# Turning K and Q in place to free 2 KB for half a streamed weight unit

One change to a tuned kernel: a memory-augmented recurrent attention whose weights do not all fit on the core.

## Chip, cores, metric

One core of a Trainium2 chip. The metric is device time in microseconds (us) of the whole kernel; lower is better. Engines are TensorE (PE; its weight loads PEld), VectorE (DVE), ScalarE (ACT), GpSimd (POOL), SyncE (SP) and 16 DMA engines. A verdict of faster or slower needs 2%.

## The reference

```python
def _A_ref(x, mem0, Wq, Wk, Wv, Wo, seg_len):       # S = 2048, Dm = 1024, H = 32, Dh = 128, M = 8, seg = 32
    mem = mem0
    for s in range(n_seg):                          # 64 segments, one after the other
        h = concatenate([mem, x[segment s]])        # 8 + 32 rows
        q, k, v = h @ Wq, h @ Wk, h @ Wv            # each Dm x (H Dh)
        p = softmax(where(mask, q k^T * scale, -1e9))
        o = (p v) @ Wo
        mem = o[:M]                                 # the next segment starts from this
        outs.append(o[M:])
# _B_ref: gelu(x @ w1 + b1) @ w2 + b2;  result: x + A(layernorm(x)) + B(layernorm(x))
```

Segments depend on each other through `mem`, and each needs all four matrices of 8 MB.

## The kernel before

The weights are 64 units of 512 KB: K, Q and V in halves of 8 units (K0, Q0, K1, Q1, V0, V1), then O with 16 units of two heads each. SBUF holds 46 of them all the time. Of the other 18, one waits in PSUM and 17 are read again from HBM in every segment, through six buffers:

```python
def start_stream():
    ...
        t = slab(STREAM_PLACES[started % STREAM_BUFS])             # one of six 4 KB-per-partition buffers
        if streams[started] == IN_PSUM and "kept" in nxt:
            ...                                                    # the unit kept in PSUM, copied by VectorE
        else:
            nc.sync.dma_start(out=t[:, :], in_=copies[streams[started]])
        stream_tiles.append(t); started += 1
def unit_done(unit):
    if IS_STREAMED[unit]:
        start_stream()                                             # a used unit's buffer takes the next transfer
        ...
```

A segment's own 32 rows are 8 memory rows and 24 rows x; the last 8 rows of four segments ("left-over rows", hL) are projected together, once per four segments, K in segments with s mod 4 = 0, Q in 1 (unit half 0) and 2 (half 1), V in 3, O in 1. I call these the first, second, third and fourth **kind** of segment. K and Q leave PSUM through one shared home, `nat_home`, and are turned from there by VectorE:

```python
def rows_out(ps, out, cp): cp(out=out, in_=ps.rearrange("p (h e) -> p h e", e=32)); let_go(ps)
def turn(out):             nc.vector.transpose(out=out, in_=nat_home)
def turn_k():              st["kT"] = sp.tile([P, 16, 32], BF16, name="kT", tag="a"); turn(st["kT"][:, :, :])
def turn_kL(ps, u):        rows_out(ps, nat_home, nc.vector.tensor_copy); kL[u] = ...; turn(kL[u][:, :, :])
def turn_q(ps):            rows_out(ps, nat_home, nc.scalar.copy); turn(q_home[:, :, NL:40])
...
psK1, psK1L = half_pass("K", 1, left_k, {})
rows_out(psK1, nat_home, nc.scalar.copy)
at = {0: [lambda: scores(0), turn_k], 6: [lambda: sums(0)]}        # after unit 0 / unit 6 of the Q1 pass
if left_k:
    at[1] = [lambda: turn_kL(psK1L, 1)]
psQ1, psQ1L = half_pass("Q", 1, left_q[1], at)
turn_q(psQ1)
```

`scores(u)` makes the products of Q and K on TensorE, the exponential `pr` on ScalarE (L745) and the mask on VectorE (L750); `sums(u)` divides by the row sums (TensorE first, L758). L628 are the products of K, Q and V, L808 those of O, L250 the cast that ends the memory's path to the next segment.

The softmax here doesn't subtract the row's maximum and nothing guards it: scores larger than these inputs give would overflow.

## Time and profile before

Runs of this kernel vary by over 1%: over four calls its single runs lie between 1996 and 2025 us, all of the same state, with medians of 2014.0, 2011.5, 2011.8 and 2011.5. A difference between two kernels of under 5 us needs the many rounds that the experiments have.

| what | before |
|---|---|
| time, median | 2014.7 us |
| TensorE busy | 1779 us, 88% |
| DMA, 600 to 1900 us | share 1.00, 383 GB/s |

In the lists of waits a row reads: engine and line, what ended the wait, total us, times, longest. In the stretches a row reads: from:to, length, then busy us and instruction count of each engine, the granted clock, DMA share, GB/s. The prediction shows the lines, and splits the 158 us for which TensorE is idle.

### The profile page before, as it was taken

To read this page: it belongs to the slowest core of one execution; us is meant where nothing else is said; L and a number is where in the kernel's file an instruction comes from. 1 tells how busy PE (TensorE), PEld (TensorE's weight loads), DVE (VectorE), ACT (ScalarE), POOL (GpSimd) and SP (SyncE) were. 2 spreads that over 40 slices of the span, in tenths; PEclk is the share of its full clock that TensorE was granted. 3 is DMA by queue.
4 is the path that set the end of the run, shared out by engine and by line. 5 is a ranking of instruction groups with operands and counts; after the bars stand their busy time and mean duration, and the time that the engine had idled before them with its cause. 6 is when DMAs were issued, how large, how long until landed. Compare 5 with 4: busy or idle time off the path is not lost.

```text
span 2011.7 us, 77091 instructions
## 1 busy us (share of the span) xinstructions
PE 1779.0 (88%) x34291; PEld 978.6 (49%) x34291; DVE 862.9 (43%) x2232; ACT 590.2 (29%) x1349; POOL 280.1 (14%) x544
## 2 busy tenths in 40 slices
PE   6999999988688988898889888888888989888887
PEld 3444444444344455545555545555545445554443
DVE  6656566333243444343434434334434343434332
ACT  4343434212222222222222222222222322222222
POOL 0000000002331111111111111111111111111111
PEclk9999999999999999999999999999999999999999
DMA  9821212779899999999999999999999999999998
GB/s 329 262 53 44 55 41 55 285 286 399 329 364 380 390 385 374 380 383 379 389 383 384 389 364 384 392 369 385 373 380 376 391 364 390 390 401 389 388 381 308
DMA packets 227402, 661.13 MB, mean 329 GB/s; under 512 B 48107, under 2 KB 63387, under 8 KB 227068
## 3 DMA queue, kind: packets, MB, share of 16 engines
q1 hardware_dynamic: 207324, 636.04, 83.5%
q0 software_dynamic: 16512, 17.92, 2.7%
q8 instruction: 268, 4.39, 0.9%
q10 hardware_dynamic: 3232, 2.25, 0.3%
q14 instruction: 66, 0.54, 0.1%
HBM read 641.85 MB, written 31.52 MB: 335 GB/s over the span
## 4 chain that ended last, share of the span: by engine, by line
PE 58%; DMA 29%; issue 5%; DVE 4%; ACT 2%; POOL 1%; SPq 0%; DVEq 0%; ACTq 0%; POOLq 0%
PE acc L628 26%; DMA u<-Wc_O 13%; PE ps L430 10%; PE acc L808 8%; PE ps L478 7%; DMA u<-Wc_V 6%; DMA res<-hr_d 3%; DMA u<-Wc_Q 2%; PE ps L511 2%; DMA outL_d<-res 2%; PE mixed L783 1%; ACT d_oL L671 1%; DVE b_oL L684 1%; DVE d_oL L671 1%; PE acc L783 1%
## 5 line engine op out<-in xcount | busy, mean ns | idle before, releaser
L628 PE MATMUL acc<-u,hr 128*32 128x512 bf16 x11520 | 792.7, 382 | 47.2 <-DMA u<-Wc_V 15.0
L628 PEld LDWEIGHTS <-hr 128*32 128x32 bf16 x12288 | 356.4, 97 | 311.1 <-issue 71.0
L671 ACT CAST d_oL<-acc 128x512 bf16<-128x512 f32 x256 | 150.3, 587 | 443.0 <-PE acc L628 354.1
L628 PE MATMUL acc<-u,hrL 128*32 128x512 bf16 x2880 | 259.6, 389 | 8.0 <-issue 8.0
L430 PE MATMUL ps<-u 128*128 128x512 bf16 x896 | 195.7, 381 | 2.6 <-ACT u L327 2.6
L808 PEld LDWEIGHTS <-b_oL 128*32 128x32 bf16 (+1 forms) x3552 | 117.0, 104 | 109.7 <-issue 76.4
L808 PE MATMUL acc<-u,d_oL 128*32 128x256 bf16 (+1 forms) x2220 | 134.2, 294 | 34.4 <-DMA u<-Wc_O 20.9
L684 DVE STREAM_TRANSPOSE kT<-d_oL 128x512 bf16<-128x512 bf16 x128 | 90.6, 708 | 160.4 <-ACT d_oL L671 157.1
L808 PE MATMUL acc<-W_O,b_oL 128*32 128x256 bf16 (+1 forms) x2220 | 135.8, 307 | 22.5 <-issue 22.5
L478 PE MATMUL ps<-u 128*128 128x512 bf16 x672 | 147.0, 379 | 0.0
L808 PEld LDWEIGHTS <-d_oL 128*32 128x32 bf16 (+1 forms) x3552 | 102.8, 98 | 86.6 <-issue 63.1
L430 PEld LDWEIGHTS <-u 128*128 128x128 bf16 x896 | 88.0, 98 | 109.0 <-issue 4.8
L808 PE MATMUL acc<-u,b_oL 128*32 128x256 bf16 (+1 forms) x1332 | 96.9, 311 | 34.7 <-DMA u<-Wc_O 28.9
L684 DVE STREAM_TRANSPOSE b_oL<-d_oL 128x512 bf16<-128x512 bf16 x128 | 91.1, 712 | 73.3 <-ACT d_oL L671 70.8
L628 PEld LDWEIGHTS <-hrL 128*32 128x32 bf16 x3072 | 89.5, 98 | 63.2 <-issue 25.0
L213 DVE COPY u<-kept 128x1024 bf16<-128x1024 bf16 x126 | 81.2, 686 | 73.5 <-PE acc L808 54.8
L796 DVE CAST b_oL<-acc 128x160 bf16<-128x160 f32 x128 | 41.6, 325 | 163.6 <-PE acc L789 163.6
L478 PEld LDWEIGHTS <-u 128*128 128x128 bf16 x672 | 65.3, 98 | 77.4 <-DVE g_u L446 0.4
L223 POOL DMA_DIRECT2D hr<-hr_d x63 | 34.6, 549 | 489.5 <-PE acc L628 405.3
L948 POOL DMA_DIRECT2D out_dram<-res x124 | 63.5, 517 | 260.3 <-DVE res L910 259.0
L438 ACT ACTIVATE g_xb<-ps,b1col 128x512 bf16<-128x512 f32 x112 | 76.9, 687 | 60.6 <-PE ps L430 59.5
L893 ACT CAST d_oL<-acc 128x256 bf16<-128x256 f32 x63 | 23.5, 372 | 235.2 <-PE acc L808 207.7
(130 smaller groups left out, 2148.9 us busy)
## 6 DMA issues: line engine op xcount, KB each, us to landing
u<-Wc_O SPq DMA_DIRECT2D x384, 512.0 KB
u<-Wc_K SPq DMA_DIRECT2D x256, 512.0 KB
u<-Wc_V SPq DMA_DIRECT2D x256, 512.0 KB
u<-Wc_Q SPq DMA_DIRECT2D x193, 512.0 KB
u<-in_B_w_dram SPq DMA_DIRECT2D x16, 448.0 KB
u<-in_B_w_dram SPq DMA_DIRECT2D x14, 512.0 KB
u<-in_A_Wq_dram SPq DMA_DIRECT2D x12, 512.0 KB
u<-in_A_Wv_dram SPq DMA_DIRECT2D x12, 512.0 KB
```

The costliest lines, as they stand in the source:

```text
L213: nc.vector.tensor_copy(out=t[:, 1024 * b:1024 * b + 1024], in_=nxt["kept"][:, b, :])
L430: nc.tensor.matmul(ps[:, :].rearrange("p (s t) -> p s t", t=SEG), lhsT=w1_sb[fb // 14 * 8 + kt][:, (fb % 14) * P:(fb % 14 + 1) * P], rhs=x ...
L438: nc.scalar.activation(out=xb[:, :], in_=ps[:, :], func=ACT.Identity, bias=b1col[:, fb:fb + 1], scale=1.0)
L478: nc.tensor.matmul(ps[:, :], lhsT=gts[fc // 4][:, fc % 4, t * P:(t + 1) * P], rhs=w2_sb[fc // 2][:, fc % 2, cs], start=(fc == 0), stop=(fc ...
L511: nc.tensor.matmul(pss[2 * t + nb][:, :], lhsT=gts[fc // 4][:, fc % 4, t * P:(t + 1) * P], rhs=w2_sb[fc // 2][:, fc % 2, nb * 512:nb * 512 ...
L628: nc.tensor.matmul(o, lhsT=lhs[:, i, :], rhs=m, start=(i == seq[0]), stop=(i == seq[-1]), tile_position=(0, 32 * j),)
L671: cp(out=out, in_=ps.rearrange("p (h e) -> p h e", e=32))
L684: nc.vector.transpose(out=out, in_=nat_home)
L783: nc.tensor.matmul(oV[b][:, c, :], lhsT=V[q, c * P:(c + 1) * P], rhs=prA[q, c, :], start=(c == 0), stop=False, skip_group_check=True, tile ...
L796: cp(out=outs[u][:, hs, NL * slot:NL * slot + 40], in_=oV[b])
L808: nc.tensor.matmul(acc[r:r + n // 8, 0:n], lhsT=lhs[:, 4 * (i % 4) + 2 * u + k, :], rhs=t[:, 1024 * k + n * jq:1024 * k + n * jq + n], sta ...
L948: nc.gpsimd.dma_start(out=out_flat[rows, 256 * j:256 * j + 256], in_=res[32 * j:32 * j + NX, :])
```

## The change

Its intent: free 2 KB per partition and keep there one of the two heads of one streamed O unit, so that 256 KB less are read per segment. K and Q are copied straight to where they will lie and turned there; V's home and the residual's buffer go, and the residual is loaded into the buffers of the softmax's weights (`pr`, `pr_last`) once these are used up.

```diff
-SCRATCH = 576
-SMALL = 3520
+SCRATCH = 512
+SMALL = 3584
+HALF = [unit for unit in ORDER[48:] if IS_STREAMED[unit]][0]
...
-    qL = nc.alloc_sbuf_tensor_at("qL", [P, 2, 16, SEG], BF16, offset=SCRATCH)
-    v_home = nc.alloc_sbuf_tensor_at("v_home", [P, 512], BF16, offset=SCRATCH + 2048)
-    pr_last = nc.alloc_sbuf_tensor_at("pr_last", [P, 224], BF16, offset=SCRATCH + 3072)
+    half_home = nc.alloc_sbuf_tensor_at("half_home", [P, DM], BF16, offset=SCRATCH)
+    pr_last = nc.alloc_sbuf_tensor_at("pr_last", [P, 256], BF16, offset=SCRATCH + 2048)
+    qL_last = nc.alloc_sbuf_tensor_at("qL_last", [P, 16, SEG], BF16, offset=SCRATCH + 2560)
...
-                nc.sync.dma_start(out=t[:, :], in_=copies[streams[started]])
+                c0 = 1024 if streams[started] == HALF else 0
+                nc.sync.dma_start(out=t[:, c0:2048], in_=copies[streams[started]])
...
-            def turn(out):
-                nc.vector.transpose(out=out, in_=nat_home)
+            def turn(ps, home, cp):
+                rows_out(ps, home, cp)
+                nc.vector.transpose(out=home, in_=home)
...
-            rows_out(psK1, nat_home, nc.scalar.copy)
+            turn_k(psK1, 1)
...
-            at = {0: [lambda: scores(0), turn_k], 6: [lambda: sums(0)]}
             if left_k:
-                at[1] = [lambda: turn_kL(psK1L, 1)]
+                turn_kL(psK1L, 1)
+            at = {0: [lambda: scores(0)], 6: [lambda: sums(0)]}
...
-                st["res"] = sp.tile([P, 256], BF16, name="res", tag=tag)       # own buffer in three kinds of four
+                st["res"] = sp.tile([P, 256], BF16, name="res", tag="e")       # the buffer of pr, always
...
+                if n == 7 and left_o:
+                    st["resL"] = pr_last
+                    nc.gpsimd.dma_start(out=st["resL"][:, :], in_=hrL_d[og, :, 256:512])
```

(Cut: the identity and masks move to other buffers; `q_left` now comes before `turn_q`.)

More of the change, by code (lines that the diff above doesn't have):

```diff
@@ L141, in slab @@
         return slabs.tile([P, 2048], BF16, name="u", tag=place)
-    ident = consts.tile([P, P], BF16, name="ident")
-    make_identity(nc, ident[:])
+    qL = [consts.tile([P, 16, SEG], BF16, name="qL"), qL_last]
+    ident = pr_last[:, 0:P]
+    make_identity(nc, ident)
+    ident_mem = consts.tile([P, 4, NL], BF16, name="ident_mem")
+    nc.vector.tensor_copy(out=ident_mem[:, :, :], in_=ident.rearrange("p (j t) -> p j t", j=4)[:, :, NX:SEG])
     bd = consts.tile([P, P], BF16, name="bd")
@@ L150 @@
         nc.vector.memset(bd[q, q], 1.0)
-    mask = qL.rearrange("p u h t -> p (u h t)")[:, 0:NX + GRP * 16]
+    mask = qL_last.rearrange("p h t -> p (h t)")[:, 0:NX + GRP * 16]
     mask_order = mask[:, 0:NX]
@@ L184 @@
     copies = {
-        unit: dram.tile([P, 2048], BF16, name="Wc_" + "_".join(map(str, unit)))[:, :]
+        unit: dram.tile([P, 1024 if unit == HALF else 2048], BF16, name="Wc_" + "_".join(map(str, unit)))[:, :]
         for unit in ORDER if IS_STREAMED[unit]
@@ L190, in fetch @@
         w, i, u = unit
-        if w == "O":
+        if unit == HALF:
+            h = 4 * i + 2 * u
+            nc.sync.dma_start(out=half_home[:, :], in_=Wo_v[:, h, :])
+            nc.sync.dma_start(out=t, in_=Wo_v[:, h + 1, :])
+        elif w == "O":
             h = 4 * i + 2 * u
@@ L237, with put_mem @@
     nat_home, q_home = outs[0][:, :, 32:64], outs[1][:, :, 24:64]
-    def put_mem(o_sb, hT, ps, nb=4, m0=0):
+    def put_mem(o_sb, hT, ps, nb=4):
         nc_ = KT // nb
-        rows = ident[:, :].rearrange("p (j t) -> p j t", j=nb)[:, :, m0 + NX:m0 + SEG]
+        rows = ident_mem[:, :, :] if nb == 4 else ident_mem[:, 1::2, :]
         psM = ps[:, 0:8 * KT].rearrange("p (c j t) -> p c j t", c=nc_, j=nb)
@@ L323, in turn_x @@
             for kt in range(KT):
-                nc.tensor.transpose(pT[:, kt, :], xn[:, kt * P:(kt + 1) * P], ident[:, :])
+                nc.tensor.transpose(pT[:, kt, :], xn[:, kt * P:(kt + 1) * P], ident)
             for half in range(2):
@@ L505 @@
                     nc.tensor.matmul(
-                        pss[n][:, :], lhsT=ident[:, :], rhs=xtoks[4 * tg + n // 2][:, cs], start=False, stop=False
+                        pss[n][:, :], lhsT=ident, rhs=xtoks[4 * tg + n // 2][:, cs], start=False, stop=False
                     )
@@ L565, in keep_unit @@
                 for k in range(4):
-                    nc.tensor.transpose(tr[:, k, :], t[:, 512 * n + P * k:512 * n + P * (k + 1)], ident[:, :])
-                turned = v_home.rearrange("p (k t) -> p k t", k=4)
+                    nc.tensor.transpose(tr[:, k, :], t[:, 512 * n + P * k:512 * n + P * (k + 1)], ident)
+                turned = late.tile([P, 512], BF16, name="VL0").rearrange("p (k t) -> p k t", k=4)
                 nc.vector.tensor_copy(out=turned, in_=tr)
@@ L570, in keep_unit @@
                     c0 = 512 * (n % 2) + P * k
-                    nc.tensor.transpose(kept[:, n // 2, c0:c0 + P], turned[:, k, :], ident[:, :])
+                    nc.tensor.transpose(kept[:, n // 2, c0:c0 + P], turned[:, k, :], ident)
             nxt["kept"] = kept
@@ L680, in left_values, with turn_k @@
                 VL[u] = values_out(ps, late.tile([P, 512], BF16, name=f"VL{u}"), nc.vector.tensor_copy)
-            def turn(out):
-                nc.vector.transpose(out=out, in_=nat_home)
-            def turn_k():
-                st["kT"] = sp.tile([P, 16, 32], BF16, name="kT", tag="a")
-                turn(st["kT"][:, :, :])
+            def turn(ps, home, cp):
+                rows_out(ps, home, cp)
+                nc.vector.transpose(out=home, in_=home)
+            def turn_k(ps, u):
+                st["kT", u] = nat_home if u else sp.tile([P, 16, 32], BF16, name="kT", tag="a")[:, :, :]
+                turn(ps, st["kT", u], nc.scalar.copy)
             def turn_kL(ps, u):
-                rows_out(ps, nat_home, nc.vector.tensor_copy)
                 kL[u] = sp.tile([P, 16, 32], BF16, name=f"kL{u}")
-                turn(kL[u][:, :, :])
+                turn(ps, kL[u][:, :, :], nc.vector.tensor_copy)
             def turn_q(ps):
-                rows_out(ps, nat_home, nc.scalar.copy)
-                turn(q_home[:, :, NL:40])
+                turn(ps, q_home[:, :, NL:40], nc.scalar.copy)
             def turn_qL(ps, u):
-                rows_out(ps, nat_home, nc.vector.tensor_copy)
-                turn(qL[:, u, :, :])
+                turn(ps, qL[u][:, :, :], nc.vector.tensor_copy)
             def q_left(u):
@@ L707, in q_left @@
                 else:
-                    q = qL[:, u, :, :][:, :, NL * i4:NL * i4 + NL]
+                    q = qL[u][:, :, NL * i4:NL * i4 + NL]
                 nc.vector.tensor_copy(out=q_home[:, :, 0:NL], in_=q)
@@ L719, in keep_q @@
                     out=qS[:, 2 * u:2 * u + n, :, :].rearrange("p i h t -> p h i t"),
-                    in_=qL[:, u, :, :][:, :, (GRP - n) * NL:].rearrange(
+                    in_=qL[u][:, :, (GRP - n) * NL:].rearrange(
                         "p h (i t) -> p h i t", i=n
@@ L725, in scores @@
             def scores(u):
-                kT, qL_ends = st["kT"], ends(q_home)
+                kT, qL_ends = st["kT", u], ends(q_home)
                 sA = mixed[:, 0:160].rearrange("p (c q) -> p c q", q=40)
@@ L743, in scores @@
                         )
-                pr = pr_last if u else sp.tile([P, 224], BF16, name="pr", tag="e")
-                nc.scalar.activation(out=pr[:, :], in_=mixed[:, 0:224], func=ACT.Exp, scale=INV_SQRT_DH)
+                pr = pr_last[:, 0:224] if u else sp.tile([P, 256], BF16, name="pr", tag="e")[:, 0:224]
+                nc.scalar.activation(out=pr, in_=mixed[:, 0:224], func=ACT.Exp, scale=INV_SQRT_DH)
                 prA = pr[:, 0:160].rearrange("p (c q) -> p c q", q=40)
@@ L805, in o_product @@
                 for k in range(2):
+                    w_k = half_home if unit == HALF and k == 0 else t[:, 1024 * k:1024 * k + 1024]
                     for jq in range(DM // n):
@@ L810, in o_product @@
                             lhsT=lhs[:, 4 * (i % 4) + 2 * u + k, :],
-                            rhs=t[:, 1024 * k + n * jq:1024 * k + n * jq + n],
+                            rhs=w_k[:, n * jq:n * jq + n],
                             start=(unit == O_UNITS[0] and k == 0),
@@ L818 @@
             psK, psKL = half_pass("K", 0, left_k, {})
-            rows_out(psK, nat_home, nc.scalar.copy)
-            turn_k()
+            turn_k(psK, 0)
             if left_k:
@@ L823 @@
             psQ, psQL = half_pass("Q", 0, left_q[0], {})
-            turn_q(psQ)
             if first:
@@ L827 @@
             q_left(0)
+            turn_q(psQ)
             if left_q[0] and not first:
@@ L831 @@
             psK1, psK1L = half_pass("K", 1, left_k, {})
-            rows_out(psK1, nat_home, nc.scalar.copy)
-            if left_k and more and not first:
-                load_left_rows(g + 1, nc.gpsimd)
-            at = {0: [lambda: scores(0), turn_k], 6: [lambda: sums(0)]}
+            turn_k(psK1, 1)
             if left_k:
-                at[1] = [lambda: turn_kL(psK1L, 1)]
+                if more and not first:
+                    load_left_rows(g + 1, nc.gpsimd)
+                turn_kL(psK1L, 1)
+            at = {0: [lambda: scores(0)], 6: [lambda: sums(0)]}
             psQ1, psQ1L = half_pass("Q", 1, left_q[1], at)
-            turn_q(psQ1)
             if first:
@@ L842 @@
             q_left(1)
+            turn_q(psQ1)
             if left_q[1] and not first:
@@ L846 @@
             psV, psVL = half_pass("V", 0, left_v, {})
-            st["V", 0] = values_out(psV, v_home, nc.scalar.copy)
+            st["V", 0] = values_out(psV, sp.tile([P, 512], BF16, name="v", tag="a"), nc.scalar.copy)
             if first:
@@ L852, with load_res @@
                 at[4].append(lambda: left_values(0, psVL))
-            if left_o:
-                def load_resL():
-                    st["resL"] = sp.tile([P, 256], BF16, name="resL", tag="rs")
-                    nc.gpsimd.dma_start(out=st["resL"][:, :], in_=hrL_d[og, :, 256:512])
-                at[3] = [load_resL]
-            def load_res(tag, eng):
-                st["res"] = sp.tile([P, 256], BF16, name="res", tag=tag)
-                eng.dma_start(out=st["res"][:, :], in_=hr_d[s + 1, :, 256:512])
-            if i4 != 1 and not final and not first:
-                at[5] = [lambda: load_res("rs", nc.gpsimd)]
+            def load_res():
+                st["res"] = sp.tile([P, 256], BF16, name="res", tag="e")
+                nc.gpsimd.dma_start(out=st["res"][:, :], in_=hr_d[s + 1, :, 256:512])
+            at[5] = [load_res]
             psV1, psV1L = half_pass("V", 1, left_v, at)
-            st["V", 1] = values_out(psV1, sp.tile([P, 512], BF16, name="v1", tag="a"), nc.scalar.copy)
+            st["V", 1] = values_out(psV1, sp.tile([P, 512], BF16, name="v", tag="a"), nc.scalar.copy)
             if first:
@@ L887 @@
                     fn()
-                if n == 7 and not st.get("res"):
-                    load_res("e", nc.scalar)
+                if n == 7 and left_o:
+                    st["resL"] = pr_last
+                    nc.gpsimd.dma_start(out=st["resL"][:, :], in_=hrL_d[og, :, 256:512])
             nw = 2 if left_o else 1
@@ L903 @@
                     lead_products(LEAD // 2)
-                put_mem(o_sb, nxt["hT"], mixed[:, 256:512], 4 // nw, m0 if left_o else 0)
+                put_mem(o_sb, nxt["hT"], mixed[:, 256:512], 4 // nw)
                 if led:
```

## The prediction

> **What bounds the kernel now.** I read the page first, then the stretches, TensorE's waits, the timeline.
>
> ```profile
> PE 1779.0 (88%) x34291; PEld 978.6 (49%) x34291; DVE 862.9 (43%) x2232; ACT 590.2 (29%) x1349; POOL 280.1 (14%) x544
> DMA  9821212779899999999999999999999999999998
> q1 hardware_dynamic: 207324, 636.04, 83.5%
> q8 instruction: 268, 4.39, 0.9%
> ```
>
> The page shows two candidates, TensorE (88% busy) and the DMA engines (90% or more in nearly every slice of the recurrence). The recurrence is 64 segments; the cast that ends each one's memory path (L250, once per segment) gives their starts, and between 600 and 1900 us a segment takes 24.25 us. So one or the other must give way by turns, and the stretches of one segment show where. This one starts at 1475.83 and is of the third kind of four (s mod 4 = 2); its stages here are Q0 with K1, then O.
>
> ```profile
> core 0: us, PE busy (x) PEld busy (x) DVE busy (x) ACT busy (x) POOL busy (x), PEclk, DMA share, GB/s
> 1477.76:1481.21 3.45, 3.45 (x68) 1.71 (x64) 1.59 (x3) 1.17 (x2) 1.13 (x3) 1.00 0.87 312
> 1489.29:1498.61 9.32, 5.67 (x168) 4.03 (x164) 2.39 (x6) 1.67 (x5) 0.54 (x1) 0.98 1.03 406
> ```
>
> In Q0 and K1 TensorE never pauses and the DMA sinks to 312 GB/s: all six stream buffers are full and the next transfer waits for a release. In O the DMA runs at 406 GB/s, which I take as its ceiling here, and TensorE is idle for 3.65 of 9.32 us. The question is whether TensorE's pauses are waits for data. Its waits between 600 and 1900 us:
>
> ```profile
> PE acc L808 <- DMA u<-Wc_O: 39.3, 74, 1.0
> PE acc L808 <- issue: 37.8, 31, 2.1
> PE acc L628 <- issue: 21.7, 24, 1.7
> PE mixed L758 <- DVE pr L750: 13.4, 17, 1.7
> PE mixed L733 <- DVE b_oL L709: 10.2, 12, 1.0
> PE acc L628 <- DMA u<-Wc_V: 9.5, 24, 0.9
> ```
>
> TensorE is idle for 158 of these 1300 us (busy 1142.1). Streamed data explain only 52 (39.3 and 9.5 above, 2.8 for Q and 0.7 for K). "issue", a pause without a releaser, explains some 77 when all its rows are added (the smaller ones are not shown). The timeline shows both kinds in an O stage, data first (third-kind segment), then issue (first kind):
>
> ```profile
> 1491.78 0.40 PE L808 MATMUL acc<-u,d_oL 128*32 128x256 bf16 x8 [0.68 <-DMA u<-Wc_O]
> 1442.16 0.62 PE L808 MATMUL acc<-u,d_oL 128*32 128x256 bf16 x15
> 1444.91 0.50 PE L808 MATMUL acc<-u,d_oL 128*32 128x256 bf16 x9 [2.13 <-issue]
> ```
>
> The second stops after 15 matmuls, in the middle of a unit of 8 whose buffer has landed. I therefore set the packet records of queue 8 beside the pauses. Queue 8 carries 268 packets of 16,384 B; times 256 that is 68,608, and TensorE ran 68,582 matmuls and weight loads: it is TensorE's instruction stream, 64 B each. All but a few of the 80 issue pauses of segments 5 to 61 (82 us) end 1.2 to 1.6 us after such a packet ends. TensorE there waits for instructions.
>
> **What the skill says.** "Runtime: NRT & Kernel Launch", section "Instruction fetch mechanics": instruction memory is refilled in 16 KiB blocks of 256 instructions by a DMA queue of the sequencer's own, and the page calls the fetch hidden. The block size agrees with queue 8; hidden it is not here, with 82 us of pauses. "DMA: Bandwidth & Descriptors", section "Queues, rings and completion order": each DMA engine goes round the queues that have work, packet by packet. So instruction blocks and small loads queue among the weights: small loads issued by GpSimd take a median of 4.9 to 5.9 us to land in this trace. The same page, "Why small descriptors are slow (HBM only)", gives a fixed overhead per packet. The trace agrees: a 4,096 B packet takes a median of 159 ns, a 2,048 B one 85 ns, so halves cost 7% more per byte.
>
> **The change, part by part.** *Half a unit stays.* HALF is the second unit of O. Its stream goes from 128 packets of 4,096 B to 128 of 2,048 B. Where the DMA is saturated, transfers land 1.30 us apart; the half takes 128 x 85 ns / 16 = 0.68 us. Saved: 0.62 us per segment, or 39 us over 63, if all of it reached the end. It can reach it only where TensorE still waits for data after HALF has passed. Adding TensorE's data waits in O, segment by segment (segments 5 to 61), and capping each at 0.62, I get a mean of 0.38 us for the first kind (instruction waits of 1.4 us lie in the same stage), 0 for the second (O carries double work there, TensorE never waits), 0.61 for the third (2.04 us of data waits, nearly all segments reach the cap) and 0.15 for the fourth (instruction waits of 1.6 us). A group of four gains 1.14 us, 15.75 groups 18 us. Two more for the waits in V of the second kind, which the head start carried over shortens. I take a quarter off (5 us), since a TensorE that waits less for data runs sooner into the instruction wait.
>
> *K and Q turned in place.* Same copies and transposes (0.59 us on ScalarE, 0.71 on VectorE); only their places and order change. The waits of ScalarE's copies on the shared home (ACT L671 behind kL or qL, 43.2 and 33.9 us) go. In the first kind the left-over K of unit 1 was turned after the mask of the scores; now VectorE does transpose 0.71, copy 0.69, transpose 0.71 ahead of it. With the copy of K1 ended at 1434.94 in one such segment, the mask ends at about 1437.5 in place of 1435.85, and the sums, made at 1436.08 without a wait, come 1.45 us later. In return the 0.8 us wait of the second scores, on L709, goes: they come at some 1440.0 in place of 1439.49. The path is 0.5 us longer; half lies under the instruction wait that follows, leaving +0.25 x 16 = 4 us. The late stop also delays the release of two stream buffers by 1.4 us, which eats 0.2 of the 0.38 gained: 3 us. In the second kind the exponential could start 1.2 us sooner, but see the next part.
>
> *Residual in the buffer of the weights.* "Weights" are the softmax's here. The residual now lies in pr in all segments, so the next segment's exponential waits until the output DMAs that read it have landed. By the trace the last lands 7.2 us after the start of a first kind (exponential at 8.2: no wait), 7.8 in a second (free at 6.5: the wait takes over what the home's wait was, sums again near 8.5, gain 0) and 5.6 in a fourth (6.1: hardly any). In the third kind this wait exists already; there the residual was loaded late by ScalarE and its sum came at 0.9 us on average in place of 0.33, so an earlier load ends it sooner: 0.2 us off, 2 us in all. The second residual, loaded late now, should land about as the first did.
>
> *Sum.* -18 - 2 + 5 + 4 + 3 - 2 = -10 us; the first four segments (the DMA at 339 to 365 GB/s with the loads of the resident weights) give 2 more. That is 2014.7 - 12 = 2002.7; I say 2000, as the next rival pulls the mean down.
>
> **The rivals.** *The DMA is the bound throughout.* For it: a DMA share of 1.00 over the 1300 us. Against: 312 GB/s in stages with TensorE full, and 77 us of pauses that no weight would end. It would give 39 us: 1975. *The instruction stream takes all.* For it: 82 us of such pauses, in the very stages where data are waited for; blocks come 4.7 us apart at the fastest. Against: third-kind O stages have five data waits in a row and little else. With it only 5 us are left and the new waits on VectorE cost as much: 2013. *The reused buffer becomes a wait.* For it: exponentials of the third kind already wait, up to 2.4 us, for outputs that read pr. If output DMAs land 1.5 us later than now, two kinds lose 1 us per segment: some +20 from my sum, 2020. Against: their landing is set by the same saturated queue as before, with fewer bytes in it.
>
> **Range and chances.** Between the instruction rival and half of the DMA rival lies most of the weight: 1984 to 2010. Faster by over 2% means under 1974.4, which needs more than the whole saving: 5%. Slower by over 2% (over 2055) needs a new wait of 0.6 us in every segment: 2%. Within 2%: 93%.
>
> **What would show it.** Queue 1 should move 262,144 B less in each segment, some 16.5 MB. TensorE's waits on Wc_O should fall by a third, issue waits stay or grow, the wait of L733 on L709 vanish, that of the sums on the mask rise by 1.4 us in the first kind, and exponentials wait on out_dram from res in the second. The prediction is wrong if issue waits fall as well (then the instruction fetch was only the sign of a full DMA), if third-kind segments gain much less than 0.6 us, or if in-place transposes take longer than 0.71 us.

## The result

The first measurement gave 1999.6 us (1996 to 2006, 4 runs) against 2014.0: a ratio of 0.9933, with a 95% interval of 0.9904 to 0.9963. Two later calls with more rounds gave 0.9968 (0.9950 to 0.9987) and 0.9965 (0.9947 to 0.9983), medians 2005.2 and 2004.3. A ratio is the mean time of one kernel's fast runs over that of the other's of the same rounds, so it is not quite the ratio of the medians quoted. The change makes the kernel some 6 to 13 us faster: clear of noise, under 2%.

The page of the changed kernel, the lines that answer to those of before:

```profile
PE 1767.1 (89%) x34271; PEld 966.9 (48%) x34291; DVE 856.2 (43%) x2233; ACT 588.6 (30%) x1349; POOL 291.0 (15%) x562
DMA  9821212679999999999999999999999999999998
q1 hardware_dynamic: 207228, 619.26, 82.6%
q8 instruction: 268, 4.39, 0.9%
```

Queue 1 moves 16.8 MB less, the bytes of the half unit (64 x 262,144 B), as foreseen. And the DMA line still reads 9 nearly everywhere. The stretches, whole first, then Q0 with K1 and O of one third-kind segment:

```profile
core 0: us, PE busy (x) PEld busy (x) DVE busy (x) ACT busy (x) POOL busy (x), PEclk, DMA share, GB/s
600.00:1900.00 1300.00, 1143.74 (x27516) 662.28 (x27516) 523.91 (x1385) 361.95 (x921) 211.96 (x397) 0.99 1.00 376
1473.21:1476.66 3.45, 3.45 (x68) 1.70 (x64) 1.60 (x3) 1.17 (x2) 1.02 (x2) 1.00 1.00 344
1485.36:1492.73 7.37, 5.07 (x168) 3.95 (x164) 2.39 (x6) 1.67 (x5) 1.09 (x2) 1.00 1.04 409
```

The share stays at 1.00 while the rate falls from 383 to 376 GB/s: the same share moves fewer bytes, and a 4,096 B packet of queue 1 takes 171 ns on average in place of 169. A share of 1.00 therefore did not say that time hangs on bytes. TensorE's waits, 600 to 1900 us:

```profile
PE acc L816 <- DMA u<-Wc_O: 43.2, 71, 2.3
PE acc L816 <- issue: 31.1, 25, 2.4
PE mixed L765 <- DVE pr L757: 22.6, 27, 1.4
PE acc L637 <- issue: 17.4, 20, 2.7
PE acc L637 <- DMA u<-Wc_V: 9.3, 25, 1.3
```

(L816 is L808 of before, L765 L758, L757 L750, L637 L628.) The wait of the second scores (L733 on L709) is gone, the wait of the sums on the mask has grown from 13.4 to 22.6 us, issue waits are about as before, and waits for Wc_O have not fallen in this profile. (Over all profiles they have, a little: 39.3 and 46.3 us in the two of before, 43.2, 35.2 and 35.6 in the three of the changed kernel.) The timeline shows the grown wait in a first-kind segment, ScalarE, VectorE and TensorE from the copy of K1 to the sums. Before, the mask (L750) came first and the left-over K after it:

```profile
1434.35 0.59 ACT L671 CAST d_oL<-acc 128x512 bf16<-128x512 f32 x1 [1.36 <-PE acc L628]
1435.07 0.36 ACT L745 ACTIVATE pr<-mixed 128x224 bf16<-128x224 f32 x1
1435.46 0.39 DVE L750 TENSOR_TENSOR pr<-pr,beside 128x96 bf16<-128x96 bf16 x2 [1.66 <-ACT pr L745]
1435.77 0.70 DVE L684 STREAM_TRANSPOSE kT<-d_oL 128x512 bf16<-128x512 bf16 x1
1436.08 0.26 PE L758 MATMUL mixed<-pr,bd 128*32 128x160 bf16 x4
1436.51 0.69 DVE L671 CAST d_oL<-acc 128x512 bf16<-128x512 f32 x1
```

In the changed kernel:

```profile
1429.46 0.59 ACT L680 CAST d_oL<-acc 128x512 bf16<-128x512 f32 x1 [2.66 <-PE acc L637]
1430.08 0.71 DVE L694 STREAM_TRANSPOSE d_oL<-d_oL 128x512 bf16<-128x512 bf16 x1 [2.23 <-ACT d_oL L680]
1430.71 0.65 DVE L680 CAST kL<-acc 128x512 bf16<-128x512 f32 x1
1431.40 0.71 DVE L694 STREAM_TRANSPOSE kL<-kL 128x512 bf16<-128x512 bf16 x1
1432.03 0.35 DVE L757 TENSOR_TENSOR pr<-pr,beside 128x96 bf16<-128x96 bf16 x2
1432.30 0.25 PE L765 MATMUL mixed<-pr,bd 128*32 128x160 bf16 x4 [0.98 <-DVE pr L757]
```

The exponential was done at 1430.46 (ACT L752, 1430.10 plus 0.36), but its mask stands behind three turning steps. In place, a transpose takes what it took before (0.71 us in the median).

ScalarE's exponential now also waits in segments that had no such wait, 8.2 us in all, of the second kind as foreseen (before there were only the 10.5 us on outL_d):

```profile
ACT pr L752 <- DMA out_dram<-res: 8.2, 7, 1.6
ACT pr L752 <- DMA outL_d<-res: 3.8, 4, 2.2
```

I measured the segments of each kind from one L250 cast to the next (segments 5 to 61). With the two profiles of before and three of the changed kernel that the experiments brought:

| kind | before, us | changed, us | difference |
|---|---|---|---|
| first | 24.66, 24.63 | 25.20, 25.30, 25.05 | +0.54 |
| second | 24.54, 24.28 | 24.20, 24.11, 24.03 | -0.29 |
| third | 23.44, 23.54 | 22.87, 23.22, 23.12 | -0.42 |
| fourth | 24.22, 23.74 | 23.45, 23.60, 23.53 | -0.45 |

One profile's mean of a kind has a standard error of 0.1 to 0.4 us, so the third is sound, the first likely, the other two rough. The sum, -0.62 us per four segments, makes -9 us over segments 5 to 61.

### The profile page after: what moved, and what is told of

Its sections match the earlier page's. It is cut to its first block, busy times and chain, and to the rows that moved or that the text cites. A ratio compares the mean times of both kernels' runs of the same rounds, so it can differ in the third digit from the quotient of the medians.

```text
span 1994.6 us, 77183 instructions
## 1 busy us (share of the span) xinstructions
PE 1767.1 (89%) x34271; PEld 966.9 (48%) x34291; DVE 856.2 (43%) x2233; ACT 588.6 (30%) x1349; POOL 291.0 (15%) x562
## 4 chain that ended last, share of the span: by engine, by line
PE 41%; DMA 24%; issue 5%; DVE 2%; POOL 1%; ACT 1%; DVEq 0%; POOLq 0%; ACTq 0%
PE acc L637 29%; DMA u<-Wc_O 13%; PE acc L816 9%; DMA u<-Wc_V 8%; DMA out_dram<-res 1%; PE mixed L790 1%; DVE d_oL L694 1%; DMA u<-Wc_Q 1%; PE acc L790 1%; PE mixed L765 1%; ACT d_oL L680 0%; DVE kL L680 0%; POOL out_dram L946 0%; PE mixed L740 0%; POOL hr_d L400 0%
## 5 line engine op out<-in xcount | busy, mean ns | idle before, releaser
L637 PE MATMUL acc<-u,hr 128*32 128x512 bf16 x11520 | 792.9, 382 | 34.2 <-DVE hr L259 12.4
L637 PEld LDWEIGHTS <-hr 128*32 128x32 bf16 x12288 | 354.7, 97 | 306.5 <-issue 58.7
L637 PE MATMUL acc<-u,hrL 128*32 128x512 bf16 x2880 | 260.1, 388 | 5.9 <-issue 5.9
L816 PEld LDWEIGHTS <-b_oL 128*32 128x32 bf16 (+1 forms) x3552 | 111.3, 99 | 119.7 <-issue 90.1
L816 PE MATMUL acc<-u,d_oL 128*32 128x256 bf16 (+1 forms) x1998 | 127.3, 294 | 20.6 <-DMA u<-Wc_O 10.8
L816 PE MATMUL acc<-u,b_oL 128*32 128x256 bf16 (+1 forms) x1332 | 92.2, 296 | 55.5 <-DMA u<-Wc_O 40.3
L816 PE MATMUL acc<-W_O,b_oL 128*32 128x256 bf16 (+1 forms) x2220 | 126.8, 292 | 12.7 <-issue 12.7
L816 PEld LDWEIGHTS <-d_oL 128*32 128x32 bf16 (+1 forms) x3552 | 101.9, 99 | 60.1 <-issue 33.9
L637 PEld LDWEIGHTS <-hrL 128*32 128x32 bf16 x3072 | 90.3, 98 | 64.6 <-issue 25.5
L862 POOL DMA_DIRECT2D res<-hr_d x64 | 35.9, 560 | 574.8 <-DVE d_oL L803 283.1
L694 DVE STREAM_TRANSPOSE kT<-kT 128x512 bf16<-128x512 bf16 x64 | 45.5, 712 | 172.2 <-ACT kT L680 172.2
L790 PEld LDWEIGHTS <-v 32*128 32x128 bf16 x2048 | 62.5, 91 | 103.2 <-issue 74.1
L694 DVE STREAM_TRANSPOSE b_oL<-b_oL 128x512 bf16<-128x512 bf16 x128 | 90.8, 709 | 48.3 <-ACT b_oL L680 48.2
L680 ACT CAST kT<-acc 128x512 bf16<-128x512 f32 x64 | 37.5, 586 | 233.6 <-PE acc L637 233.6
L680 ACT CAST b_oL<-acc 128x512 bf16<-128x512 f32 x128 | 75.4, 589 | 81.1 <-PE acc L637 79.6
```

Of the source, the lines that this page charges most:

```text
L637: nc.tensor.matmul(o, lhsT=lhs[:, i, :], rhs=m, start=(i == seq[0]), stop=(i == seq[-1]), tile_position=(0, 32 * j),)
L694: nc.vector.transpose(out=home, in_=home)
L790: nc.tensor.matmul(oV[b][:, c, :], lhsT=V[q, c * P:(c + 1) * P], rhs=prA[q, c, :], start=(c == 0), stop=False, skip_group_check=True, tile ...
L816: nc.tensor.matmul(acc[r:r + n // 8, 0:n], lhsT=lhs[:, 4 * (i % 4) + 2 * u + k, :], rhs=w_k[:, n * jq:n * jq + n], start=(unit == O_UNITS[ ...
L862: nc.gpsimd.dma_start(out=st["res"][:, :], in_=hr_d[s + 1, :, 256:512])
```

## Experiments

The theory: TensorE is the bound most of the time, and waits for weights only in part of the O stages; elsewhere it waits for its own instructions or for VectorE. Rivals: the DMA is the bound throughout; instruction waits take whatever data waits leave; the reused buffers are a new wait. Kernels that are wrong on purpose passed the comparison with the reference all the same, so passing says nothing about them; the attention's part in the output seems too small for it. All profiled runs compared are fast, but for one (the last).

**The changed kernel again**, as the yardstick of its call.

> The changed kernel once more, as the yardstick of this call. Its first measurement was a ratio of 0.993 with single runs from 1996 to 2006 us. Expected 0.991 to 0.996 again; outside that, differences of under 10 us between kernels of different calls mean nothing.

Ratio 0.9968, 2005.2 us median of 22 runs (1995 to 2019): just outside the 0.991 to 0.996 expected, and less of a gain than the first four runs showed. By the rule set there, differences of under 10 us between kernels of different calls prove nothing; I say where I compare across calls.

**The half unit alone**, in the kernel before:

```diff
-                nc.sync.dma_start(out=t[:, :], in_=copies[streams[started]])
+                c0 = 1024 if streams[started] == HALF else 0
+                nc.sync.dma_start(out=t[:, c0:2048], in_=copies[streams[started]][:, c0:2048])
...
-                            rhs=t[:, 1024 * k + n * jq:1024 * k + n * jq + n],
+                            rhs=t[:, 1024 * k0 + n * jq:1024 * k0 + n * jq + n],   # k0 = 1 for HALF, else k
```

> The kernel before with one part of the change alone: the second unit of O is streamed with half its bytes (both heads of that unit use the same half, so the result is wrong on purpose); nothing is turned in place and no buffer moves. My theory (TensorE waits for data in some O stages only, elsewhere for instructions or for itself): 10 to 22 us faster than before, nearly all in segments of the third kind (0.4 to 0.6 us each) and some in the first. Rival 1, the DMA is the bound throughout: 35 to 40 us faster, in all four kinds. Rival 2, instruction waits fill what data waits leave: under 6 us faster.

Ratio 0.9911 (0.9879 to 0.9943), 1993.3 us: 18 us faster than before, inside the theory's 10 to 22 and half of what rival 1 needs. The third kind went to 23.05 us, its O stage from 8.28 to 7.84. Its other kinds are no shorter than before in that profile, which was of its slowest run, so where the rest lies it does not tell. Its waits:

```profile
PE acc L811 <- issue: 33.5, 29, 2.4
PE acc L811 <- DMA u<-Wc_O: 32.5, 60, 1.5
```

(L811 is L808 of before.) Here, without the rest of the change, waits for Wc_O do fall, from 39.3 (46.3 in the second profile of before) to 32.5 us. The first kind's O is hardly shorter, 7.57 us beside 7.63 (standard error 0.2).

**The buffers alone**: the changed kernel with `HALF = None`.

> The changed kernel with the half unit undone: all bytes are streamed as before, but K and Q are turned in place and the residual lies in the softmax's buffers. My theory: first-kind segments lose 0.5 us or more (the scores' mask of unit 0 is held up by the turning of the left-over K), second-kind gain 0 to 0.3, third-kind gain 0.2 to 0.4, fourth no change: 0 to 6 us slower than before in all. Rival 1 (DMA the bound throughout, so that the parts on VectorE do not matter): within 2 us of before. Rival 3 (the reused buffers cost a wait): 15 us slower or more, with waits of the exponential on output DMAs in all kinds.

Ratio 1.0034 (1.0016 to 1.0052), 2018.5 us: 7 us slower than before, 1 us outside what I had expected and clear of both rivals. The first kind takes 25.17 us. In the third the exponential's late start is gone (the wait of the sums fell from 0.42 and 0.32 us to nothing), yet the kind takes 23.53 us as before: its waits for data took the place, 2.91 us in that profile against 2.48 and 2.73. The parts add up: 18 faster and 7 slower make 11, and the whole change measured 6 to 13.

**The left-over K turned after the mask**, in the changed kernel:

```diff
-                turn_kL(psK1L, 1)
             at = {0: [lambda: scores(0)], 6: [lambda: sums(0)]}
+            if left_k:
+                at[1] = [lambda: turn_kL(psK1L, 1)]
```

> The changed kernel with one thing moved: in first-kind segments the left-over K of unit 1 is turned after the mask of unit 0's scores, not before it. My theory: the 1 us wait of the sums on the mask in that kind goes, the kind shortens by 0.5 to 1.0 us, and the kernel is 6 to 16 us faster than the changed one. Rival: the stop hides under the waits for data and instructions in O that follow; then the wait goes but O waits longer by as much, and the time stays within 3 us of the changed kernel.

Ratio 0.9905 (0.9882 to 0.9928), 1994.0 us: 13 us faster than the changed kernel of the same call (0.0063 of 2011). The same timeline:

```profile
1427.65 0.59 ACT L680 CAST d_oL<-acc 128x512 bf16<-128x512 f32 x1 [2.66 <-PE acc L637]
1428.27 0.71 DVE L694 STREAM_TRANSPOSE d_oL<-d_oL 128x512 bf16<-128x512 bf16 x1 [2.23 <-ACT d_oL L680]
1428.91 0.35 DVE L757 TENSOR_TENSOR pr<-pr,beside 128x96 bf16<-128x96 bf16 x2
1429.18 0.68 DVE L680 CAST kL<-acc 128x512 bf16<-128x512 f32 x1
1429.33 0.26 PE L765 MATMUL mixed<-pr,bd 128*32 128x160 bf16 x4
```

The mask comes before the left-over K and the sums start without a wait. The lists of TensorE's waits have two rows that moved in opposite ways (31.1 to 36.2 and 35.2 to 43.2 us in the three profiles of the changed kernel):

```profile
PE acc L816 <- issue: 39.7, 33, 2.4
PE acc L816 <- DMA u<-Wc_O: 31.2, 59, 1.1
```

Both waits of the first kind are now gone, that of before (on L709) and that of the change: VectorE's 0.91 to 0.98 us there is zero.

**late_kl and the changed kernel once more**, on another chip.

> late_kl once more, as the yardstick of this call and to see whether its gain repeats: ratio to the kernel before 0.988 to 0.993, and 6 to 16 us faster than the changed kernel of this call. If the gain of the first call was chance: within 4 us of the changed kernel.

> The changed kernel a third time, on the chip of this call: ratio to the kernel before 0.993 to 0.997, as both times before.

Ratios 0.9918 (0.9892 to 0.9943) and 0.9965 (one slow run of the changed kernel left out): 9 us apart. The gain repeats. The first kind, though, takes 24.77 and 25.13 us in the two profiles of late_kl, only 0.24 less than in the changed kernel on average, where 10 us would be 0.6 us in each of 16 segments; the profiles' scatter does not let me place the rest. In O of the first kind data waits fell from 1.29, 0.78 and 0.89 us to 0.64 and 0.28, but issue waits rose from 1.22, 1.61 and 1.50 us to 1.72 and 2.24, and O got no shorter (8.19 us, 7.95 in the changed kernel). Over all of segments 5 to 61 the waits on VectorE for scores and sums fell by 13 us and data waits by 8, and issue waits rose by 13: 8 us less in all, about the measured gain. So the rival that expected O to take the saving back was right in part.

**The left-over Q turned after the mask too:**

```diff
-                turn_qL(psQL, 0)
...
+            elif left_q[0]:
+                at[1] = [lambda: turn_qL(psQL, 0)]
```

> The kernel late_kl with one thing more moved: in second-kind segments the left-over Q of unit 0 is turned after the mask of unit 0's scores, not before the turning of K1. VectorE then reaches the mask 1.4 us sooner, so the mask waits only for the exponential, and that for the output DMAs that read the residual. My theory: the wait of the sums in the second kind falls from 0.57 us to 0.2 to 0.4 (the DMA wait takes over part), 3 to 6 us faster than late_kl. Rival (the reused buffer has fully taken the place of the home's wait): no change of the wait, within 2 us of late_kl. Against the kernel before: ratio 0.986 to 0.990.

Ratio 0.9908 (0.9878 to 0.9938), 1993.6 us: no faster than late_kl in its two calls (others than this one), though intervals of 0.6% do not exclude the 3 us expected. The wait itself fell as expected, from 0.57 to 0.29 us, but V1 of that kind took 4.14 us (standard error 0.24) in place of 3.75 and 3.60. The expected gain was not seen: I had counted a shortened wait as time.

**The half unit not streamed at all:**

```diff
+SKIP = [HALF]
-        if started < len(streams):
+        if started < len(streams) and streams[started] in SKIP:
+            stream_tiles.append(low["low0"])
+            started += 1
+        elif started < len(streams):
```

> The changed kernel with the half unit not streamed at all (a resident tile stands in its place; wrong on purpose): 256 KB less per segment than the changed kernel, 512 KB less than before. My theory: 6 to 16 us faster than the changed kernel, less than the 39 us that its bytes take at the DMA's full rate; third kind gains most. Rival 1 (DMA the bound): 35 us or more. Rival 2 (instruction waits fill up): under 5 us, issue waits grow by as much as data waits fall.

Ratio 0.9907 (0.9872 to 0.9941), 1994.3 us. Against the changed kernel's three ratios, all of other calls, that is 5 to 12 us faster. So 256 KB per segment, 39 us of the DMA at its full rate, are worth 18 us in the kernel before (half_only), 13 us between buffers_only and the changed kernel of the same call (1.0034 and 0.9968), and 5 to 12 us here. (The skipped unit also leaves its buffer to the next one, so this is a little more than bytes alone.) In its profile, of its slowest run, data waits are 5 us below the changed kernel's average and issue waits 9 us above it (segments 5 to 61): what the second rival had expected, though two profiles of the kernel before lie 10 us apart in issue waits.

**The DMA unloaded**: as above, with all streamed units of V and O in `SKIP`.

> The changed kernel with all streamed units of V and O replaced by a resident tile (wrong on purpose): 7 transfers per segment are left, so the DMA engines are under half busy and TensorE can't wait for weights. The question is what the issue waits do. Theory a, the instruction blocks are slow because they queue in saturated DMA engines: a block arrives sooner, the issue waits of 1.4 us per segment fall under 0.3, segments take 21.8 to 22.5 us, the kernel 1880 to 1920 us. Theory b, TensorE runs through 256 instructions faster than the fetch can ever follow: issue waits stay at 1.4 us or grow, segments take 23 us or more, the kernel 1940 to 1985 us.

1886.1 us (0.9373). Data waits are gone, and the waits of TensorE between 600 and 1800 us are:

```profile
PE acc L820 <- issue: 49.8, 31, 3.2
PE mixed L769 <- DVE pr L761: 19.8, 27, 1.0
```

(L820 is O.) The whole, and then K0 to V1 and O of one third-kind segment:

```profile
600.00:1800.00 1200.00, 1109.88 (x27206) 651.54 (x27205) 509.46 (x1369) 357.16 (x912) 205.18 (x385) 0.98 0.54 179
1384.84:1397.33 12.49, 12.49 (x320) 6.81 (x316) 6.88 (x20) 4.53 (x11) 4.62 (x9) 1.00 0.68 194
1397.33:1405.49 8.16, 6.17 (x168) 4.67 (x164) 2.30 (x6) 1.67 (x5) 1.11 (x2) 0.79 0.54 208
```

Neither theory holds alone. The time fell as theory a had it, since 22.3 us per segment is TensorE's own 20.6 and little else. The issue waits stayed as theory b had it: 1.22 us per segment against 1.45 before, but now nearly all in O, where 1.56, 0.30, 2.25 and 0.83 us fall to the four kinds, and none in K0 or the end of a segment. The full DMA did delay most instruction blocks: a block's packet starts a median of 3.1 us after TensorE begins the block before it in the kernel before, and 1.1 us here (a block's edge is where the pauses lie, see below). But the blocks that ended a pause were no earlier here (3.4 us, 3.5 before). Why those come late with the DMA half free stays open. O of the second kind fits an O that outruns its instructions: there a unit takes half of them, some 202 in 8.2 us against 328 in 6.7 to 8.3, and in before it had no issue wait at all.

**Fewer instructions in O**, in late_kl:

```diff
-                            start=(c == 0), stop=False, ...
+                            start=(c == 0), stop=bool(u), ...
-                    for b in range(2):
+                    for b in range(0 if u else 2):
```

> late_kl with the left-over keys left out of the two value steps that lie in O (wrong on purpose): 32 matmuls of 16 columns and 32 weight loads less per segment, 64 of some 330 instructions of that stage, a quarter of an instruction block; no DMA, no other engine and no other stage changes. These matmuls take TensorE about 0.4 us per segment (32 records some 12 ns apart beside their neighbours). Theory b (TensorE runs through its instruction blocks faster than they come): a quarter of a block at 4.7 us per block is 1.2 us, so issue waits in O fall by 0.5 us or more in kinds 1, 3 and 4 and the kernel is 20 to 50 us faster than late_kl, part of it given back to data waits. Rival (the issue pauses have another cause, or data waits take their place at once): issue waits fall by under 0.2 us or data waits rise as much, and the kernel is 0 to 15 us faster, no more than the matmuls' own time.

Ratio 0.9823 (0.9792 to 0.9854), 1975.4 us: 19 us faster than late_kl of that call. I had counted twice: the records show 296 instructions in O in place of 328, 16 matmuls and 16 loads, not 64. Issue waits in O went from 1.72 and 2.24 us (the two profiles of late_kl) to 1.40 in the first kind, from 0.75 and 0.55 to 0.65 in the third, and from 1.23 and 1.34 to 0.90 in the fourth. In O of the second kind, where TensorE waits for next to nothing, the stage shortened by 0.20 us, from 8.07 to 7.87: that is the matmuls' own time, some 13 us over the kernel. Some 6 us are left for the instruction stream, within the intervals. Over segments 5 to 61 issue waits fell from 90.7 and 88.6 us to 63.9, but data waits rose from 44.5 and 49.4 to 64.6, as the rival had it. At 19 us the time lies between the theory (20 to 50) and the rival (0 to 15). The run speaks for theory b in the waits; most of what it freed went to data waits.

**Residuals in buffers of their own**, in buffers_only:

```diff
-                st["res"] = sp.tile([P, 256], BF16, name="res", tag="e")
+                st["res"] = half_home[:, 0:256]
-                    st["resL"] = pr_last
+                    st["resL"] = half_home[:, 256:512]
```

> The kernel buffers_only (all bytes streamed, K and Q in place) with the residuals in buffers of their own, in the 2 KB that the half unit leaves free there. My theory: the exponential's waits on output DMAs go in all kinds; third-kind segments gain 0 to 0.3 us, the second nothing, as VectorE's turning still holds the mask, the others nothing: 0 to 6 us faster than buffers_only, ratio to before 1.000 to 1.004. Rival 3 (the reused buffer is what buffers_only lost): ratio 0.996 or less.

Ratio 1.0009 (0.9991 to 1.0027), 2015.1 us: 5 us faster than buffers_only, though in another call and with intervals that overlap. It is inside what was expected and clear of the third rival's 0.996: by these runs the reused buffers cost 5 of the 7 us that buffers_only lost, not the 15 and more of that rival. The waits of the exponential on output DMAs are gone. What I had not expected is the second kind: the wait of the sums fell from 0.60 to 0.30 us there, although VectorE still turns the left-over Q first. late_both took the other cause away and it fell to 0.29. Each cause holds about half of the wait.

**The kernel before once more**, for a second profile.

> The kernel before once more, for a second profile: the segment lengths by kind rest on one profile of it so far (24.66, 24.54, 23.44 and 24.22 us). If each repeats within 0.3 us, differences of 0.4 us and more between kernels that several profiles show are the kernels' own; if not, only sums over kinds can be compared.

A single look, 2003.7 us beside 2003.1 for the same kernel (state unknown, as for single runs). The kinds took 24.63, 24.28, 23.54 and 23.74 us: three within 0.3 of the first profile, the fourth 0.48 off.

## Why the prediction was right, and where a step failed

*The time*: 2000 predicted, 1999.6 measured in its call, 2004 to 2005 in the later ones; all in the range. By cause, errors did not make each other good: the two parts of the sum, bytes and buffers, were each tried alone and each came out near its term (bytes -15 against -18, buffers about +5 against +7). By kind they did: the terms give +0.07, -0.13, -0.81 and -0.15 us per segment, and +0.54, -0.29, -0.42 and -0.45 were measured. The first and third kind did worse, the second and fourth better, so that the sum came this close is in part luck.

*Bytes*: -18 - 2 + 5 = -15 us predicted, -18 (interval -12 to -24) measured in half_only. That the saving is about half of the 39 us or less is shown three times: in half_only, between buffers_only and the changed kernel, and in skip_half. The cap by data waits, segment by segment, was the step that decided this; that the saving falls where the cap put it is shown for the third kind alone. In the list of waits of the changed kernel the third less on Wc_O did not come (38.0 us on average of three profiles, 42.8 in before), since the rest of the change adds data waits (Wc_O 47.7 us in buffers_only).

*Turning, first kind*: this step failed in size. I put it at +0.07 us in all (0.25 for the path and 0.2 for the late release, less 0.38 of data gain); the kind grew by 0.54. The stop of the sums came, at Q1, which grew from 2.16 to 3.37 us (mean of the profiles; 1.2 us where I had 1.45). V1 gave nearly all of it back, 4.08 to 2.99: these stages together are only 0.1 us longer, and K0 is 0.17 longer, within its scatter. The loss lies after them: O takes 7.95 us in place of 7.63 (standard error 0.1 of the difference). The term that did not come is the gain of 0.38 us from bytes in O. With the buffers changed, O takes 7.90 us with all bytes (buffers_only) and 7.95 with half the unit gone; in the kernel before, 7.63 and 7.57 (half_only); each of the single profiles has a standard error of 0.2. The late release, put at 0.2, is near the 0.3 that O lost. By what path O lost it is not shown: data waits rose from 0.78 to 0.99 us and issue waits from 1.25 to 1.44, both within scatter. And when late_kl removed the stop, data waits in O fell to 0.46 us, issue waits rose to 1.98 and O stayed long, while the kernel became 9 to 13 us faster.

*Turning, second kind*: no gain from the home's wait, as predicted; the sums' wait stayed at 0.57 us (0.60 before). That two causes hold about half of it each is what own_res and late_both show, with one profile each.

*Residual, third kind*: the wait went, but its 2 us did not come; in buffers_only data waits filled the place.

*Fourth kind*: 0.15 us predicted, 0.45 measured, with profiles of before 0.48 apart. Open.

*Instructions*: in the changed kernel issue waits neither fell with the bytes nor took all the gain (77.4, 75.5 and 76.2 us in segments 5 to 61, before 82.5 and 72.7); in late_kl and fewer_instr they and the data waits do give to each other. That they are waits for instructions was read from the packets alone. The place of the pauses settles it: if TensorE's recorded instructions are counted in order, all 80 pauses of before fall on three neighbouring places of every 256; so do the 75 of the changed kernel's first profile and the 44 of light, each on three of their own. light shows that they are not only the sign of a full DMA.

*Readings that were off*: blocks are not 4.7 us apart "at the fastest"; that is the fifth percentile, and the closest are 3.6 us apart. A 2,048 B packet takes 84 ns in the median, and by their means (86 and 171 ns on queue 1 in the changed kernel, 600 to 1900 us) halves cost no more per byte. Small loads by GpSimd take 5.4 to 5.9 us; 4.9 us is an output. 0.2 us in 16 segments is 3 us and not 2. None of these moves the sum by more than 2 us.

**A version faster than both**: late_kl, at 0.9905 and 0.9918 of the time before, against 0.9933 to 0.9968 for the change.

## What to carry to other kernels

A DMA share of 1.00 does not price a byte: add the consumer's data waits stretch by stretch, cap the saving with them, and read pauses without a releaser as a bound of their own. When a reorganised buffer lets work be done earlier, ask what stands behind it in the engine's order: three turning steps of VectorE ahead of one mask cost 9 to 13 us, at least half of the 18 that the freed memory brought. A delay is not hidden because later waits follow it: the O stage behind this one grew as well. And waits for data and for instructions take each other's place: in fewer_instr some 26 us of the one gone left some 18 us more of the other.

## What the Trainium skill lacked or had wrong

- "Runtime: NRT & Kernel Launch", section "Instruction fetch mechanics", calls the fetch hidden. Here TensorE had 80 pauses without a releaser, 82 us in segments 5 to 61, nearly all ending 1.2 to 1.6 us after a 16,384 B packet of its instruction queue and all on the same three places of every 256 instructions; with the DMA engines at a share of 0.54 there were still 1.22 us per segment.
- No page says that streams of weights slow the instruction blocks. A block's packet started a median of 3.1 us after TensorE began the block before it at a DMA share of 1.00, and 1.1 us at 0.54.
- "DMA: Bandwidth & Descriptors", section "Why small descriptors are slow (HBM only)", gives no time per packet for 2 KB against 4 KB: medians of 84 and 159 ns here, means of 86 and 171, so by the means no more per byte.
- No page gives the time of VectorE's 32x32 transpose in place ("VectorE: DVE Perf Modes", section "The three transpose paths", has one time, for 128x128): 128x512 bf16 took 711 to 712 ns in the median of each group, as from one buffer to another (708 to 712).
